# Two keys to a partition: regrouped V gathers, V table and weight transfers in a block-sparse attention and MoE kernel, with a new transfer model in its planner

## The chip, the cores and the metric

The kernel runs on one core of a Trainium2 chip. A core has the engines TensorE (PE in the profile, its weight loads PEld), VectorE (DVE), ScalarE (ACT), GpSimd (POOL) and SyncE (SP), each with its own queue of instructions that it works off in order, and 16 DMA engines that all queues of transfers share. The metric is the device time of one execution in microseconds, the lower the better; a kernel's time is the median of its runs.

## The reference

Block-sparse attention (4 batches, 8 heads, 768 positions of 64 values, blocks of 32 keys) is followed by a two-layer network on the joined heads:

```python
scores = (q @ k.T) / sqrt(64)            # per batch and head
mask   = |blk_i - blk_j| <= 1, or blk_i or blk_j is the first or the last block,
         or blk_j is one of the 3 sampled blocks of blk_i
attn   = softmax(where(mask, scores, -1e9));  a = attn @ v
x = a.transpose(0, 2, 1, 3).reshape(3072, 512)
h = x @ w_in                              # 512 x 2048
out = (h * sigmoid(beta * h)) @ w_out     # 2048 x 512, float32
```

All inputs are float32 in DRAM, the block numbers integers. Which keys a block of queries attends to is known only at run time, through the sampled blocks.

## The kernel before

**Attention.** Of 24 query blocks per batch the first and the last attend to all keys ("global"). The other 22 are worked in 11 pairs per batch, numbered 0 to 43. Each query block of a pair attends to 8 key blocks (first, last, three sampled, three neighbours), 256 keys. For a pair n the steps are, by their names in the code:

- kg (L521, POOL): copies the sampled K blocks from the transposed table KT into KG; kn (L525 on, POOL or DVE): copies first, last and neighbour blocks. 3 KG buffers.
- vv (L550, SP) reads the sampled block numbers into registers; vg (L582, SP) gathers V from a table VT in DRAM into VG, with 7 transfers to a pair (9 where a batch begins or ends). 4 VG buffers, so vg of pair n waits for av of pair n-4.
- vres (L589 on, POOL or DVE): in pairs 1 to 3 of a batch, copies the first and last block's V from pair 0's buffer.
- sc (L600, L610, PE): mask and scores, into two PSUM banks; mx (L621, DVE): row maxima; ex (L629, ACT): exponentials; rc (L635, DVE); nrm (L641, POOL or DVE): normalisation; tp (L653, PE): eight 128x128 transposes; ptv (L657, DVE): out of PSUM; av (L668, PE): times V; xv (L257, L259): out of PSUM into xT.

The global blocks have the same steps under gs, gm, ge, gr, gn, gt, gptv, gav and gx (L690 to L780).

**Tables.** For each batch K, Q and V are loaded (batch 0 by SP, L388, ahead of all; later batches by POOL, L443, into two staging buffers RAW), rearranged to fp16 by DVE (cast, vperm, perm), K and Q transposed by PE (trK, trQ, L463) and copied out of PSUM (evK, evQ). V goes back to DRAM as the table VT by SP: batch 0 in two halves of 512 B rows (vtab0.0, vtab0.1; L490), later batches at once in rows of 6 KB (vtab1 to 3; L494). Later batches are loaded in the order V, K, Q.

**MoE.** The 24 x 128 tokens are worked in 8 groups G of 256 or 512 tokens. Per group: h (L817, PE), 16 chunks of 128 hidden units by 4 matmuls; tanh (L823, ACT); stt (L828, DVE); y (L845, PE), 4 parts of 4 matmuls for each 128 tokens; oe (L263, ACT); od (output transfer, ACT). Weights are loaded by POOL, float32 to fp16 on the way, in 16 transfers: win (L417), 8 of 64 rows by 8 KB; wout (L423), 8 of 64 rows by 8 KB, four rows of w_out to a partition. All h wait for all eight win. The hidden units are therefore read at a stride of four: `w_in_v = w_in_sb[:, :, :].rearrange("x c (q p i) -> x c q i p", p=P, i=4)`.

**Order.** The kernel is written as tasks with an engine (or a choice of engines), a duration, dependencies and a priority. `Plan.run` plays them through in its own model when the kernel is built: whenever an engine is free it takes the ready task of the least priority number. The result is one order, and every engine's queue is that order cut down to the engine. In the model a transfer goes through one ring that serves one transfer after another (`ring_at = max(ring_at, end + 0.6) + t.dma`), transfers of SP and ACT also through 8 lanes in turn; a POOL load with `bulk` is held back while the ring is booked more than 3.2 us ahead. PSUM has 8 banks; `Plan(8, 4)` lets MoE tasks hold four of them while attention lasts. On the chip the order is fixed and every instruction waits for what it needs.

Of the kernel before, what the change touches and what calls it, by code (L numbers as in the profile page):

```python
# [22 lines left out]
class Task:  # L23
    def __init__(self, name, eng, dur, emit, deps=(), prio=0.0, lat=0.0,
                 opens=(), closes=(), moe=False, dma=0.0, slack=0.0, hw=0, bulk=None):
# [5 lines left out]
        self.slack, self.hw, self.bulk = slack, hw, bulk  # L31
        self.kind = name.rstrip("0123456789.")
        self.end = None


class Plan:
# [14 lines left out]
    def run(self):  # L51
# [16 lines left out]
        ring_at = 1.0  # L68
        lanes = [0.0] * 8
# [18 lines left out]
        while done < len(tasks):  # L88
            progress = False
            for e in engines:  # L90
# [3 lines left out]
                for t in waiting[e]:  # L94
# [7 lines left out]
                    if t.bulk is not None and ring_at > now + t.bulk + 1e-9:  # L102
                        continue
# [26 lines left out]
                if t.hw:  # L130
                    at = now
                    for _ in range(t.hw):
                        at = max(at, lanes[issued % 8]) + t.dur / t.hw
                        ring_at = max(ring_at, at + 0.4) + t.dma / t.hw
                        end = lanes[issued % 8] = ring_at + 0.9
                        issued += 1
                    free[e] = at
                elif t.dma:
                    ring_at = max(ring_at, end + 0.6) + t.dma
                    end = ring_at + 1.1  # L140
                t.start, t.end = now, end
                order.append(t)
                heapq.heappush(events, (end, seq, t))
                seq += 1
# [8 lines left out]
            for e in engines:  # L153
                nxt += [ready_at[t] for t in waiting[e] if ready_at[t] > now + 1e-9]
                nxt += [ring_at - t.bulk for t in waiting[e]
                        if t.bulk is not None and ring_at - t.bulk > now + 1e-9]
            nxt += [f for f, _ in bank_free if f > now + 1e-9]
            if not nxt:
                raise RuntimeError("plan is stuck: " + ", ".join(
                    t.name for e in engines for t in waiting[e]))  # L160
            now = max(now, min(nxt))
            while events and events[0][0] <= now + 1e-9:
# [3 lines left out]
                done += 1  # L166
                for s in succ.get(t, ()):
# [15 lines left out]
def kernel(  # L183
# [52 lines left out]
    VG = [sb(f"VG{i}", [P, 2, 2, D_MODEL]) for i in range(NVG)]  # L236
# [13 lines left out]
    plan = Plan(8, 4)  # L250
# [39 lines left out]
    t_sbl = add("sbl", "ACT", 0.5, emit_sbl, prio=-200, dma=0.3, hw=1)  # L290
# [46 lines left out]
    for part, f in enumerate((emit_mask0, emit_mask1, emit_mask2)):  # L337
# [9 lines left out]
    beta_row = osb[0][0:4, :]  # L347
    ident32 = t_sb[1][0:4, 0:8].bitcast(FP32)
    FQ = N_FFC // 4
    t_beta0 = add("beta", "ACT", 0.5, lambda: nc.scalar.dma_start(  # L350
        out=beta_row, in_=moe_beta.rearrange("(q x) -> q x", q=FQ)), prio=-140, dma=0.1, hw=1)
    t_id32 = add("id32", "DVE", 0.2, lambda: nc.vector.tensor_copy(
        out=ident32, in_=identity[0:4, 0:4]), deps=[t_ident], prio=-64)

    def emit_betaT():
        for i in range(4):
            nc.tensor.transpose(out=bank("beta")[:, i * FQ:(i + 1) * FQ],
                                in_=beta_row.rearrange("q (p i) -> q i p", i=4)[:, i, :], identity=ident32)
# [3 lines left out]
        out=beta_sb[:, :].rearrange("x (q i) -> x i q", i=4),  # L362
        in0=bank("beta")[:, 0:N_FFC].rearrange("x (i q) -> x i q", i=4),
# [22 lines left out]
    for i, (nm, t, dst) in enumerate((("K", k, K16), ("Q", q, Q16), ("V", v, None))):  # L386
        for f in range(2):
            tl = add(f"ld{nm}0.{f}", "SP", 0.47, lambda i=i, t=t, f=f: nc.sync.dma_start(  # L388
                out=stage_half(i, f) if i < 2 else v_stage[:, f * HH:(f + 1) * HH, :],
                in_=src6(t, 0, f * HH, HH)), prio=-80 + i * 2 + f, dma=2.0, hw=1)  # L390
# [17 lines left out]

    w_in_r = moe_w_in.rearrange("(c p) f -> c p f", p=P)
    w_out_r = moe_w_out.rearrange("(q p i) m -> q p (i m)", p=P, i=4)  # L410
    w_in_v = w_in_sb[:, :, :].rearrange("x c (q p i) -> x c q i p", p=P, i=4)
    t_win, t_wout = [], []
    THR = 3.2
    for c in range(4):
        for f in range(2):
            ps = slice(64 * f, 64 * f + 64)
            t_win.append(add(f"win{c}.{f}", "POOL", 0.85, lambda c=c, ps=ps: nc.gpsimd.dma_start(  # L417
                out=w_in_sb[ps, c, :], in_=w_in_r[c, ps, :]),
# [485 lines left out]
```

## Time and profile before

| | before |
|---|---|
| median of 3 runs | 324.45 us (322.56, 324.45, 332.4) |
| profiled execution | 323.59 us, of which the span 321.8 |
| mean granted TensorE clock | 0.929 |
| busy: PE, DVE, ACT, POOL | 280.7, 246.7, 216.8, 187.5 us |
| DMA | 42,211 packets, 43.97 MB |
| queue q1 (SP's transfers) | 27,760 packets, 25.71 MB, 27.1% of 16 engines |
| queue q0 (POOL's transfers) | 10,784 packets, 11.27 MB, 23.4% |
| V gathers, 32.0 KB each by the page's count | 268, median 2.6 us from issue to landing |

The page gives for each engine the busy tenths in 40 slices of the span; for each queue its packets, megabytes and the time that the packets took as a share of 16 engines' span; for each DMA issue the median time to landing. A timeline row reads: start, duration, engine, line, operation, out<-in, count, and in brackets the engine's idle time just before and what ended it. A row of the chain of work that ended last is start, duration, what. A group's row is busy time and the mean of one in ns, then idle time before it. TensorE's rows overlap, so its throughput is read from start to start. Every packet is also recorded in the trace with queue, size, start and duration; sizes are those stored for q0, whose loads turn float32 into fp16, and 16 packets of 4 bytes go with each transfer.

### The profile page before, as it was taken

How to read it: one execution, taken by the hardware profiler on the slowest of the kernel's cores; microseconds unless marked ns; L12 is line 12 of the kernel's file. 1: busy time of each engine (PE TensorE's matmuls, PEld its weight loads, DVE VectorE, ACT ScalarE, POOL GpSimd, SP SyncE). 2: the span in 40 equal slices, each digit the busy share in tenths (PEclk: the TensorE clock that was granted, in tenths of full speed). 3: DMA queues.
4: the chain of work that ended last, by engine and by line, in shares of the span. 5: the costliest groups of instructions: out<-in, count | busy, mean ns of one | idle time of the engine just before them, and what ended most of it. 6: DMA issues, size and time to landing. Idle time of an engine off the chain costs nothing.

```text
span 321.8 us, 10665 instructions
## 1 busy us (share of the span) xinstructions
PE 280.7 (87%) x3525; PEld 177.3 (55%) x3525; DVE 246.7 (77%) x572; ACT 216.8 (67%) x644; POOL 187.5 (58%) x528
## 2 busy tenths in 40 slices
PE   0845578989979699988979999999999999999994
PEld 0612366956755486556635656555665555554671
DVE  2996579878869989999987667999979975771060
ACT  1676435864968489789687669977679864772361
POOL 2479956848778456798966654756948453200000
PEclk9975557999979989999979999999999999999999
DMA  7889995998697586323777973335232333100201
GB/s 255 332 172 208 229 227 105 187 252 177 132 204 145 164 212 114 107 80 94 125 146 168 226 170 93 88 84 153 94 118 69 91 110 100 33 3 33 98 2 66
DMA packets 42211, 43.97 MB, mean 137 GB/s; under 512 B 6440, under 2 KB 37672, under 8 KB 42156
## 3 DMA queue, kind: packets, MB, share of 16 engines
q1 hardware_dynamic: 27760, 25.71, 27.1%
q0 software_dynamic: 10784, 11.27, 23.4%
q10 hardware_dynamic: 3612, 6.30, 5.4%
q8 instruction: 28, 0.46, 0.6%
q14 instruction: 27, 0.22, 0.2%
HBM read 45.10 MB, written 9.44 MB: 169 GB/s over the span
## 4 chain that ended last, share of the span: by engine, by line
PE 60%; DMA 14%; DVE 12%; ACT 6%; issue 3%; SPq 3%; POOL 1%; POOLq 0%; ACTq 0%; DVEq 0%
PE bank L845 22%; PE bank L817 21%; DMA VG<-VT 6%; PE bank L668 4%; PE bank L653 4%; DMA RAW<-in_k_dram 3%; DMA VT<-Vn 3%; SPq L582 3%; DVE ST L621 2%; ACT PP L629 2%; PE bank L463 2%; DVE g L828 2%; PE bank L610 2%; PE bank L600 2%; DMA sbl<-in_sampled_blocks_dram 1%
## 5 line engine op out<-in xcount | busy, mean ns | idle before, releaser
L641 POOL TENSOR_SCALAR PP<-PP,ST 128x256 f16<-128x256 f16 x168 | 81.3, 501 | 47.9 <-DVE ST L635 42.4
L629 ACT ACTIVATE PP<-bank,ST 128x256 f16<-128x256 f32 x176 | 81.6, 478 | 30.1 <-DVE ST L621 21.5
L817 PE MATMUL bank<-xT,w_in_sb 128*128 128x256 f16 (+1 forms) x512 | 97.1, 338 | 3.9 <-ACT PP L629 1.1
L845 PE MATMUL bank<-w_out_sb,g 128*128 128x512 f16 x384 | 90.9, 380 | 0.0
L828 DVE SCALAR_TENSOR_TENSOR g<-t,bank 128x512 f16<-128x512 f16 (+1 forms) x128 | 66.6, 546 | 22.1 <-ACT t L823 21.3
L823 ACT ACTIVATE t<-bank,beta_sb 128x512 f16<-128x512 f32 (+1 forms) x128 | 69.9, 589 | 14.3 <-PE bank L817 11.6
L817 PEld LDWEIGHTS <-w_in_sb 128*128 128x128 f16 x512 | 55.3, 116 | 30.1 <-issue 8.6
L521 POOL COPY KG<-KT 128x64 f32 x264 | 54.6, 256 | 24.6 <-PE bank L610 17.8
L621 DVE TENSOR_REDUCE ST<-bank 128x2 f32<-128x512 f32 x88 | 57.5, 678 | 7.5 <-PE bank L610 7.4
L845 PEld LDWEIGHTS <-g 128*128 128x128 f16 x384 | 34.7, 98 | 38.6 <-issue 4.1
L668 PE MATMUL bank<-PT,VG 128*128 128x64 f16 x704 | 31.8, 199 | 7.9 <-DMA VG<-VT 5.9
L668 PEld LDWEIGHTS <-VG 128*128 128x128 f16 x704 | 28.3, 102 | 16.5 <-issue 9.6
L629 ACT ACTIVATION_READ_ACCUMULATOR PP<-bank,ST 128x1 f32 x176 | 36.8, 209 | 0.0
L653 PE MATMUL bank<-identity,PP 128*128 128x128 f16 x352 | 30.9, 233 | 6.6 <-ACT xT L257 2.4
L653 PEld LDWEIGHTS <-PP 128*128 128x128 f16 x352 | 24.6, 104 | 15.9 <-issue 4.1
L657 DVE COPY PT<-bank 128x1024 f16<-128x1024 f16 x44 | 30.1, 684 | 4.1 <-PE bank L653 3.3
L259 DVE CAST xT<-bank 64x256 f16<-64x256 f32 (+1 forms) x52 | 20.6, 402 | 12.3 <-PE bank L668 7.5
L263 ACT ACTIVATE osb<-bank 128x512 f32<-128x512 f32 x24 | 14.4, 601 | 20.7 <-PE bank L845 20.7
L257 ACT CAST xT<-bank 64x256 f16<-64x256 f32 (+1 forms) x52 | 17.4, 346 | 15.4 <-DVE xT L259 6.3
L610 PE MATMUL bank<-KG,QT 64*32 64x256 f16 x704 | 20.9, 293 | 1.4 <-POOL KG L521 1.0
L726 ACT ACTIVATE PG<-bank,SG 128x384 f16<-128x384 f32 x32 | 18.4, 583 | 4.9 <-DVE SG L721 4.1
L600 PE MATMUL bank<-maskr,ones 64*32 64x192 f16 (+1 forms) x352 | 14.9, 272 | 5.7 <-ACT PP L629 5.5
(79 smaller groups left out, 256.6 us busy)
## 6 DMA issues: line engine op xcount, KB each, us to landing
VG<-VT SPq DMA_DIRECT2D x268, 32.0 KB, 2.6
VG<-VT SPq DMA_DIRECT2D x40, 192.0 KB, 2.9
out_dram<-osb ACTq DMA_DIRECT2D x20, 256.0 KB, 2.2
RAW<-in_v_dram POOLq DMA_DIRECT2D x6, 384.0 KB, 5.1
RAW<-in_k_dram POOLq DMA_DIRECT2D x6, 384.0 KB, 5.6
VT<-Vn SPq DMA_DIRECT2D x3, 768.0 KB, 6.1
RAW<-in_q_dram POOLq DMA_DIRECT2D x6, 384.0 KB, 6.5
w_in_sb<-in_moe_w_in_dram POOLq DMA_DIRECT2D x8, 256.0 KB, 5.9
```

Source lines behind the costliest of these rows:

```text
L521: nc.gpsimd.tensor_copy(out=kg32[:, g, :, (2 + r) * W:(3 + r) * W], in_=kt32[:, :, bass.ds(vals[3 * g + r], W)])
L610: nc.tensor.matmul(bk[u][hp * BLK:(hp + 1) * BLK, g * 256:(g + 1) * 256], lhsT=QT[b % 2][u * D:(u + 1) * D, hp, (i0 + g) * BLK:(i0 + g + 1 ...
L621: mx[n, u] = add(f"mx{n}.{u}", "DVE", 0.6, lambda n=n, u=u, sb_=sb_: nc.vector.tensor_reduce(out=sb_[:, 0, 2 * u:2 * u + 2], in_=bank(("S" ...
L629: nc.scalar.activation(out=pb[:, u, g, :], in_=bank(("S", n, u))[:, g * 256:(g + 1) * 256], func=AF.Exp, bias=sb_[:, 0, 2 * u + g:2 * u + ...
L641: (nc.vector if eng == "DVE" else nc.gpsimd).tensor_scalar(out=pb[:, u, g, :], in0=pb[:, u, g, :], scalar1=sb_[:, 2, 2 * u + g:2 * u + g + ...
L653: nc.tensor.transpose(out=o[:, s * P:(s + 1) * P], in_=pb[:, u, g, c * P:(c + 1) * P], identity=identity)
L657: ptv[n] = add(f"ptv{n}", "DVE", 0.61, lambda n=n: nc.vector.tensor_copy(out=PT[n % NPT], in_=bank16(("T", n))), deps=[tp[n]] + ([av[n - N ...
L668: nc.tensor.matmul(o[:, (g * NHP + hp) * 64:(g * NHP + hp + 1) * 64], lhsT=vgb[:, g, c, hp * P:(hp + 1) * P], rhs=pt[:, g, c, :, hp * BLK: ...
L817: nc.tensor.matmul(o[:, 0:TW], lhsT=w_in_v[:, c, f // 4, f % 4, :], rhs=xT[:, c, c0:c0 + TW], start=(c == 0), stop=(c == NHP - 1))
L823: lambda G=G, f=f, TW=TW, tt=tt: nc.scalar.activation(out=tt[:, 0:TW], in_=bank(("H", G, f))[:, 0:TW], func=AF.Tanh, bias=0.0, scale=beta_ ...
L828: lambda G=G, f=f, TW=TW, tt=tt, gg=gg: nc.vector.scalar_tensor_tensor(out=gg[:, f, 0:TW], in0=tt[:, 0:TW], scalar=1.0, in1=bank(("H", G, ...
L845: nc.tensor.matmul(o[:, :], lhsT=gg[:, f, s * P:(s + 1) * P], rhs=w_out_sb[:, f, :], start=(f == 0), stop=(f == N_FFC - 1))
```

## The change

- **V gathers.** A partition of VG now holds two neighbouring keys (2 KB in one row of the table) instead of one: a block of 32 keys takes 16 partitions, all 8 blocks of a query block stand in 128 partitions, and the second index of VG is the parity of the key instead of the lower or upper half. The same number of transfers per pair moves the same bytes. The transposes tp read the softmax at a stride of two, so that the keys' order fits. vres copies 32 partitions by 2,048 elements instead of 64 by 1,024.
- **V table.** Batch 0 is written by one transfer in rows of 6 KB, after both halves are cast.
- **Weights.** win: 8 transfers of 128 rows by 4 KB, the first half of the hidden units first; wout: 8 transfers of 128 rows by 4 KB, two rows of w_out to a partition. Chunks h.0 to h.7 wait for the first four win, h.8 to h.15 for the other four. Strides of four become two, also for beta.
- **Loads of later batches** come in the order K, Q, V; V uses K's staging buffer, after K is rearranged.
- **Planner.** Each queue of transfers (SP, ACT, POOL) has its own ring; the heads of the rings share the DMA engines packet by packet, in proportion to their packets' times. SP and ACT wait for a free lane of 8. POOL's `bulk` threshold is 2.2 us of its own ring's backlog. MoE tasks may hold five banks. With these the order of all engines changes. In the planned order vtab1 stands on SP ahead of the gathers of pairs 11 to 14, vtab2 ahead of those of pair 20, and permV1.1 on DVE ahead of stt1.6; all 12 vres go to DVE (before, 5 went to POOL).

```diff
-                 opens=(), closes=(), moe=False, dma=0.0, slack=0.0, hw=0, bulk=None):
+                 opens=(), closes=(), moe=False, dma=None, slack=0.0, bulk=None):
...
+class Rings:
+    START = {"SP": 0.4, "ACT": 0.4, "POOL": 1.0}
+    LAND = {"SP": 0.9, "ACT": 0.9, "POOL": 2.0}
...
+    def step(self):
+        live = [r for r in self.q if self.q[r] and self.q[r][0][0] <= self.at + 1e-9]
+        later = [self.q[r][0][0] for r in self.q if self.q[r] and r not in live]
+        total = sum(self.q[r][0][2] for r in live)
+        ends = [self.at + self.q[r][0][1] * total / self.q[r][0][2] for r in live]
+        return live, total, min(later + ends, default=None)
...
-                    if t.bulk is not None and ring_at > now + t.bulk + 1e-9:
+                    if t.bulk is not None and rings.backlog("POOL") > t.bulk:
+                        continue
+                    if t.dma and e != "POOL" and lanes[issued % 8] is not None:
                         continue
...
-    VG = [sb(f"VG{i}", [P, 2, 2, D_MODEL]) for i in range(NVG)]
+    VG = [sb(f"VG{i}", [P, 2, 2 * D_MODEL]) for i in range(NVG)]
...
-    plan = Plan(8, 4)
+    plan = Plan(8, 5)
...
-    w_out_r = moe_w_out.rearrange("(q p i) m -> q p (i m)", p=P, i=4)
-    w_in_v = w_in_sb[:, :, :].rearrange("x c (q p i) -> x c q i p", p=P, i=4)
+    w_out_r = moe_w_out.rearrange("(q p i) m -> p q (i m)", p=P, i=NI)
+    w_in_v = w_in_sb[:, :, :].rearrange("x c (q p i) -> x c q i p", p=P, i=NI)
     t_win, t_wout = [], []
-    THR = 3.2
...
-                out=w_in_sb[ps, c, :], in_=w_in_r[c, ps, :]),
-                deps=[tch], prio=-50 + 0.2 * c + 0.1 * f, dma=1.3, bulk=THR))
...
+    THR = 2.2
+    for f in range(2):
+        fs = slice(f * D_FF // 2, (f + 1) * D_FF // 2)
+        for c in range(NHP):
+            t_win.append(add(f"win{f}.{c}", "POOL", 0.6, lambda c=c, fs=fs: nc.gpsimd.dma_start(
+                out=w_in_sb[:, c, fs], in_=w_in_r[c, :, fs]),
+                deps=[tch], prio=-50 + 0.1 * len(t_win), dma=(8, 0.174), bulk=THR))
...
-            for nm, t, raw, dst in (("V", v, RAW[0], Vn[b % 2]), ("K", k, RAW[1], K16), ("Q", q, RAW[0], Q16)):
+            for nm, t, raw, dst in (("K", k, RAW[1], K16), ("Q", q, RAW[0], Q16), ("V", v, RAW[1], Vn[b % 2])):
...
-                vtab[0].append(add(f"vtab0.{f}", "SP", 0.45, lambda cs=cs, vt_rows=vt_rows: nc.sync.dma_start(
-                    out=vt_rows[:, :, cs], in_=Vn[0][:, :, cs]),
-                    deps=[vperm[0][f]], prio=-64, dma=1.3, hw=1))
+            vtab[0].append(add("vtab0", "SP", 0.45, lambda vt_rows=vt_rows: nc.sync.dma_start(
+                out=vt_rows, in_=Vn[0]), deps=vperm[0], prio=-64, dma=(8, 0.234)))
...
+        HB, W2 = BLK // 2, 2 * D_MODEL
+        def two(rows):
+            return rows.rearrange("(k t) m -> k (t m)", t=2)
...
             if i0 + 1 < NB - 2:
-                yield 0.6, lambda v: (
-                    vgb[BLK:P, :, 1, :],
+                yield 6, lambda v: (
+                    vgb[5 * HB:P, :, :],
                     bass.AP(tensor=vt.tensor, offset=vt.offset + (i0 - 1) * BLK * D_MODEL,
-                            ap=[[D_MODEL, 3 * BLK], [BLK * D_MODEL, 2], [1, D_MODEL]]))
+                            ap=[[W2, 3 * HB], [BLK * D_MODEL, 2], [1, W2]]))
...
-                for r, (c, s) in enumerate(((0, 2), (0, 3), (1, 0))):
-                    yield 0.1, lambda v, g=g, r=r, c=c, s=s: (
-                        vgb[s * BLK:(s + 1) * BLK, g, c, :], vt[bass.ds(v[3 * g + r], BLK), :])
+                for r in range(3):
+                    yield 1, lambda v, g=g, r=r: (
+                        vgb[(2 + r) * HB:(3 + r) * HB, g, :], two(vt[bass.ds(v[3 * g + r], BLK), :]))
...
-                h64 = src[0:2 * BLK, 0:1, 0, :]
-                copy_on(eng, vgb[0:2 * BLK, :, 0, :], h64.to_broadcast([2 * BLK, 2, D_MODEL]))
-            vres = add(f"vres{n}", {"POOL": 0.9, "DVE": 0.5}, None, emit_vres,
+                copy_on(eng, vgb[0:BLK, :, :], src[0:BLK, 0:1, :].to_broadcast([BLK, 2, 2 * D_MODEL]))
+            vres = add(f"vres{n}", {"POOL": 1.9, "DVE": 0.7}, None, emit_vres,
...
+            pk = pb[:, :, :, :].rearrange("x u g (k c) -> x u g c k", c=2)
...
-                                            in_=pb[:, u, g, c * P:(c + 1) * P], identity=identity)
+                                            in_=pk[:, u, g, c, :], identity=identity)
...
-                            lhsT=vgb[:, g, c, hp * P:(hp + 1) * P],
+                            lhsT=vgb[:, g, c * D_MODEL + hp * P:c * D_MODEL + (hp + 1) * P],
...
-            th = add(f"h{G}.{f}", "PE", 4 * (TW / 2400.0 + 0.003), emit_h, deps=xdeps + t_win,
+            th = add(f"h{G}.{f}", "PE", 4 * (TW / 2400.0 + 0.003), emit_h, deps=xdeps + t_win[f // 8 * 4:f // 8 * 4 + 4],
```

## The prediction

> **What bounds the kernel now.** I read the page's slices first, then the DMA queues, the timeline of each engine over the first 60 us, and the table by stretches.
>
> ```profile
> PE   0845578989979699988979999999999999999994
> DVE  2996579878869989999987667999979975771060
> PEclk9975557999979989999979999999999999999999
> DMA  7889995998697586323777973335232333100201
> q1 hardware_dynamic: 27760, 25.71, 27.1%
> q0 software_dynamic: 10784, 11.27, 23.4%
> ```
>
> A slice is 8.0 us. Three stages show. Up to slice 6 (54 us) TensorE is busy 0 to 8 tenths, its clock is at half from 20 to 51 us, and the DMA engines are full. From 54 to about 176 us TensorE and VectorE are both near full. From 176 us to the end TensorE has no holes: nothing but less matmul work shortens that stage, but whatever comes earlier moves all of it. The change does not touch the matmul count, so it pays only in the first two stages.
>
> What ends the waits in the first stage, by the timelines of VectorE and TensorE, the chain, and the DMA view from 15 to 55 us:
>
> ```profile
> 38.14 0.42 DVE L259 CAST xT<-bank 64x256 f16<-64x256 f32 x1 [3.09 <-PE bank L668]
> 36.11 0.53 PE L668 MATMUL bank<-PT,VG 128*128 128x64 f16 x7 [1.36 <-DMA VG<-VT]
> 37.25 0.79 PE L668 MATMUL bank<-PT,VG 128*128 128x64 f16 x8 [0.61 <-DMA VG<-VT]
> 47.34 0.56 PE L668 MATMUL bank<-PT,VG 128*128 128x64 f16 x7 [0.79 <-DMA VG<-VT]
> ...
> 17.85 8.90 DMA VT<-Vn
> 30.33 6.78 DMA VG<-VT
> ...
> q0 software_dynamic: 1453, 4.33, 60.8%
> q1 hardware_dynamic: 4210, 2.89, 24.9%
> VG<-VT SPq DMA_DIRECT2D x33, 32.0 KB, 5.2
> ```
>
> VectorE stands 3.09 us at the first output copy because av0 has no V; V is late because the V table took 8.90 us to write and the gathers behind it 6.78 us to land, against 2.6 us for such a gather over the whole run. Weights (q0) hold 60.8% of the engines, gathers and table 24.9%.
>
> **The V table.** The trace's packet records give medians of 27 ns for 512 B, 46 for 1,024, 65 for 1,536, 84 for 2,048 (the output's) and 238 for 6,144 on the queues of SP and ACT: about 8 ns and 37.5 ns a KB. Batch 0's table goes from 1,536 packets of 27 ns (41.5 us of engine time) to 128 of 238 ns (30.5): 11/16 = 0.7 us. It also leaves in one piece, behind the second cast, which has one K copy group fewer ahead of it (kn2, half of a row of 1.24 us: 0.6). The later tables, written this way, took 6.1 us to landing (median). So 17.8 - 0.6 + 6.1 = 23.3 us instead of 26.75: 3.4 us earlier.
>
> **The gathers.** Per pair 24 packets of 46 ns on each engine become 12 of 84: 1.10 to 1.01 us, 0.1 us per pair, 4.2 us over 44 pairs. The gain under load is larger: between two gather packets an engine serves weight packets of 324 ns; these read 8 KB; one that reads 4 KB is bounded by half of that (162) and by twice the output's 2,048 B packet (168); I take 165. Between 30 and 45 us the records show gathers at 0.25 of the engines and weights at 0.79: 2.2 gather packets to one weight packet. The first pair has 32 packets per engine now, 16 after: at the same ratio 32 x 46 + 14.5 x 324 = 6.2 us (6.7 observed) becomes 16 x 84 + 7.3 x 165 = 2.6; one to one, 16 x 249 = 4.0. Issue of its nine transfers stays (3.5 us). So pair 0 has V at 23.3 + 3.5 + 2.6 to 4.0, and an estimated 1 us for the landing: 30.4 to 31.8, not 37.1. By then tp2 (32.9 now) is the last thing ahead of av0: V is no longer what it waits for.
>
> **Weights.** 1,024 packets of 324 ns become 2,048 of 165: 20.7 to 21.1 us of all engines, +0.4. POOL still issues 16; a POOL transfer took 536 to 608 ns with 64 rows and 780 with 512, so 128 rows add at most 0.1 us each. Covered: the last weight landed near 48 us, the first second-layer matmul is at 66.0. The first-layer chunks 0 to 7 now need four transfers, not eight; all eight had landed by 36, so this gains nothing itself.
>
> **The residue copy (vres).** It now writes 32 partitions by 2,048, not 64 by 1,024.
>
> ```profile
> L259 DVE COPY VG<-VG 64x1024 f16<-64x1024 f16 x7 | 3.1, 452 | 0.0
> L259 POOL COPY VG<-VG 64x1024 f16<-64x1024 f16 x5 | 5.4, 1073 | 2.4 <-PE bank L668 2.4
> ```
>
> The new order puts all 12 on VectorE. Bounds per copy: 0.45 us (partitions free) and 0.90 (twice the elements); a 128x1536 copy took 0.61 to 0.90, so 0.80. 12 x 0.80 - 3.1 = +6.5 us. Four neighbour copies (0.4) and one normalisation (1.2) leave VectorE, so its sum grows by about 4 us and POOL's falls by 1 to 2.
>
> **Transposes of the softmax (L653)** read their weights at a stride of 2. Start to start the strided L745 (stride 6) and the packed L653 both run at 56 ns at full clock; only the load's latency differs, 125 against 98 ns. Nothing to 0.03 us per pair; I take nothing.
>
> **The new order.** Instruction lists of both kernels, weighted with the durations above: ahead of the first-layer matmul h0.0 VectorE has 4 us less to do (kn2, kn3, nrm1, nrm5, mx7 go elsewhere or later), TensorE 1.4 us less (tp5, tp6, av4 come after), POOL the same. POOL bounds it: K gather 7 ends at 12.45 + 28 us of its own rows + 2 of waits = 43, then scores, av3 and the copy, 46 to 47 instead of 53.7. But by the last element-wise step of the third MoE group (126 us now) the lists are level again: VectorE -0.8 us, TensorE within 2.4, ACT 0. So what is gained is the idle time removed, not the head start:
>
> - VectorE's idle behind missing V: 3.09 + 0.40 + 0.63 = 4.1 us (timeline to 54 us; 8.3 idle in all).
> - Batch 1's K is loaded first, not third: its wait of 1.81 us (71.60) goes, counted at half, 0.9, since V then comes last.
> - Lists: 0.8.
> - Against: waits in the new places; nearest are the six of 0.4 to 0.6 us that VectorE has in that stage for other causes. I take three, 1.5; bounds 0 and 4.
>
> Sum -4.1 - 0.9 - 0.8 + 1.5 = -4.3 us. From 176 us on, nothing hides or returns it: VectorE is busy 13 to 19 of 20 us there and its extra 4 us lie beside TensorE.
>
> **Batch 1's V** is the wait that is added. Its second load stands on POOL behind the K gathers of pairs 11 and 12, which wait for K's transposes; its cast on VectorE stands ahead of stt1.6; its table on SP stands ahead of the 30 gathers of pairs 11 to 14, which av11 to av14 wait for. From K ready: 2.4 (two K gathers) + 0.8 + 5.1 (load) + 0.8 (cast) + 6.1 (table) + 3.8 (nine issues) + 2.6 to 4.7 = 21.6 to 23.7, plus 1.5 to bring K out of PSUM. TensorE has 21.2 us of work between the last K transpose and av11, and took 27.4 for the like stretch before (72.56 to 99.94). 27 is over 25, so no stall; at no stalls of its own it would wait 2 to 4 us.
>
> The profiled execution took 323.59 us (span 321.8), close to the median of 324.45. 323.6 - 4.3 = **319.3, said as 319**; own range 316 to 323 (new waits 0 to 4, the copies 0.45 to 0.90). Two per cent, 6.5 us, is about what a measurement tells from no change.
>
> **Rivals.** (a) *The head start carries.* If VectorE's idle of 8.3 us before the first MoE group shrinks as the lists allow and TensorE is the limit all along: 53.7 - 46.5 = 7.2, less 1.4 deferred; plus K's wait 1.8 and av10's wait for V of 1.48 at 91.66: 9.1, **314.5**. For it: TensorE is busy 17 to 19 of 20 us. Against: VectorE 18 to 19.4 of 20 from 100 to 160. 0.27.
>
> (b) *V late in batch 1.* Stall 2 to 4 us at av11 and at stt1.6, eating the gain: **322 to 324**. 0.18.
>
> (c) *Slower: narrow gathers.* The six 16-partition moves of a pair put one packet on each engine, all into 16 partitions. If these partitions take data slower than the engines send it, a packet holds its engine. Price from rows: in quiet bursts of 32-row gathers (201 to 206 us) the slowest packets took 230 to 310 ns; if all 2 KB packets took 0.3, a pair costs 12 x 0.3 = 3.6 us instead of 1.0. Some 13 pairs fall where the DMA engines are 0.85 to 1.0 booked (20 to 105 us): +34 us on a stretch with 13 free, so up to 20 late, half of it on the path: **330**, between 326 and 340. It decides from 0.19 us a packet (13 x 12 x 0.11 = 17: the 13 free plus the 4 gained). Against: 32-row gathers' packets, on half as many partitions as a full load's, lie on the same line (46) as the wide ones. 0.12. The Trainium skill, "SBUF — State Buffer", section "Door 1: The DMA port swizzle", says DMA bandwidth depends on how many of 16 ports the partitions reach: 32 partitions reach 8, 16 reach 4. By its 436 GB/s for all ports a 32 KB gather would need an estimated 0.30 us, not 0.15, which would be case (c). The median of 46 ns shows no such limit at 8 ports; no run yet shows 4.
>
> (d) *Rows not joined*, gathers still in 1 KB packets: V table and order alone, **322**. Against: source and target rows are both contiguous, and the output's 2,048 B rows are single packets. 0.03. The forecast has 0.40.
>
> Faster by over 2% (under 317.1): (a) and a quarter of the forecast, 0.27 + 0.10 = 0.37. Within 2%: the rest of the forecast, (b) and (d), 0.30 + 0.18 + 0.03, less 0.07 for an order that goes wrong at a place I have not seen: 0.44. Slower: (c) and those 0.07: 0.19. Range 310 to 330: it leaves out half of (c) and the ends of (a).
>
> **What would show it.** q1 with about 17,700 packets, q0 about 11,800; a 2 KB gather packet at 84 ns; VT landed by 24; no V wait at av0; h0.0 near 46 to 48 us; VectorE some 4 us busier; av11 without a wait on VG. Wrong if gather packets take over 150 ns, if VT takes as long as now, if POOL waits long for K in batch 1, or if TensorE's holes between 60 and 176 us (12 us) grow by more than 4.

## The result

| | before | after |
|---|---|---|
| median | 324.0 us (runs made beside after) | 339.8 us |
| profiled execution | 323.6 us (span 321.8) | 337.9 us (span 336.1) |
| ratio after/before | | 1.041 [1.029, 1.052] |

The changed kernel is slower by 4%, 20.8 us above the forecast and 9.8 above the top of the range. Ratios leave out disturbed runs, which the medians contain, so in what follows ratios and traces are compared, not medians.

The slices and queues of the page of after, which answer to those of before:

```profile
PE   1746859998695999976999979994999998999994
DVE  2977777879795998994999658975859983673070
PEclk9975556999998799997999989998999999999999
DMA  7879996997775685147687843413323313400101
q1 hardware_dynamic: 17632, 25.71, 25.8%
q0 software_dynamic: 11808, 11.27, 23.2%
```

A slice is now 8.4 us. The queues have the packets that were forecast. What is new stands where nothing was expected: TensorE's row, which in before was full from 169 us on, has a 4 in its 28th slice (227 to 235 us). As a mean the granted clock is the same, 0.923 against 0.929.

The starts of some matmul tasks, in us from the start of the span, tell where the time goes. h2.0 is the first first-layer chunk of MoE group 2, h2.15 its last, h4.0 and h5.0 start groups 4 and 5, y7.1.3 is the last task of TensorE:

| | h0.0 | h1.0 | h2.0 | h2.15 | h4.0 | h5.0 | y7.1.3 |
|---|---|---|---|---|---|---|---|
| before | 53.7 | 78.9 | 107.0 | 126.7 | 192.2 | 234.6 | 316.2 |
| after | 50.0 | 75.9 | 103.1 | 127.2 | 195.8 | 247.7 | 330.9 |

Up to 103 us the change leads by 3 to 4 us, near the 4.3 that the forecast has as its net gain. Then it loses 4.4 by 127 us, 3.1 more by 196, 9.5 more by 248 and 1.6 to the end.

The chain of waits of after, at the first and the last of these places (start, duration, what):

```profile
99.04 0.50 ACT osb L309
99.56 3.03 DMA out_dram<-osb
102.61 0.32 SPq L634
...
104.61 0.32 SPq L634
104.92 0.05 issue
104.97 0.04 SPq L634
105.10 3.20 DMA VG<-VT
108.31 0.14 issue
108.44 0.58 PE bank L720 x8
```

```profile
228.28 2.10 DMA VG<-VT
230.39 0.03 issue
230.41 0.02 DVEq L305
230.43 0.04 issue
230.48 1.28 DVE VG L305 x2
```

At 108.44 TensorE's av12 waits for gathered V. That gather was issued only at 105.10, since SP's queue stood: its first gather was released by the landing of an *output* transfer, at 102.59, which ScalarE had issued at 99.56 and which has no data in common with it. At 230.48 VectorE's vres waits for a gather issued at 228.28; ahead of it SP's queue had stood from 224.02 to 227.85, until the output had landed that ScalarE issued at 225.81. So what does SP's queue wait for? The waits of SP, summed by releaser (us in total, times, longest), of before and then of after, the rows that name outputs:

```profile
SPq L899 <- DMA out_dram<-osb: 51.9, 4, 34.5
SPq L582 <- DMA out_dram<-osb: 8.1, 4, 4.2
```

```profile
SPq L634 <- DMA out_dram<-osb: 48.4, 14, 9.7
SPq L951 <- DMA out_dram<-osb: 42.0, 3, 28.0
```

L899 and L951 are the kernels' ends, where SP waits for all outputs, and mean nothing. L582 and L634 are the gathers: in before they stood for outputs 4 times and 8.1 us, in after 14 times and 48.4.

**Why a gather waits for an output.** The compiled programs show it. Every transfer of SP and of ScalarE signals its landing on one of eight semaphores, and these are dealt out in turn: in the one list in which the program names the instructions of all engines, the n-th such transfer takes semaphore n modulo 8, in each of the kernels here without exception. It is not issued before the transfer eight places earlier has landed. If that one is an output, SP waits for ScalarE to get to it and then for its landing, and behind the waiting gather stand all others, for SP works in order. The places are fixed when the program is compiled, and the engines' own orders don't tell them: the first outputs stand at 76, 84, 116, 124, 156, 170, 171, 218 in before, and at 73, 80, 96, 108, 140, 151, 153, 203 in after. The earlier an output stands among the gathers, the more SP, which runs ahead of the other engines, has to wait for it. Why the list comes out otherwise for the changed transfers is not shown here.

### The profile page after: what moved, and what is told of

The parts are those of the page before. It is cut to its first block, busy times and chain, and to the rows that moved or that the text cites. A ratio compares the mean times of both kernels' runs of the same rounds, so it can differ in the third digit from the quotient of the medians.

```text
span 336.1 us, 10650 instructions
## 1 busy us (share of the span) xinstructions
PE 286.8 (85%) x3523; PEld 173.5 (52%) x3523; DVE 245.4 (73%) x567; ACT 216.5 (64%) x644; POOL 189.5 (56%) x533
## 4 chain that ended last, share of the span: by engine, by line
PE 45%; DMA 20%; DVE 15%; ACT 10%; issue 5%; SPq 4%; ACTq 0%; DVEq 0%
PE bank L869 19%; PE bank L897 14%; DMA VG<-VT 13%; ACT PP L680 5%; DMA out_dram<-osb 5%; SPq L634 4%; DVE ST L672 4%; PE bank L720 4%; PE bank L705 3%; DVE g L880 2%; ACT t L875 2%; DVE PT L709 1%; DMA g<-in_k_dram 1%; DMA VT<-Vn 1%; PE bank L661 1%
## 5 line engine op out<-in xcount | busy, mean ns | idle before, releaser
L692 POOL TENSOR_SCALAR PP<-PP,ST 128x256 f16<-128x256 f16 x172 | 83.6, 502 | 63.8 <-DVE ST L686 56.1
L869 PE MATMUL bank<-xT,w_in_sb 128*128 128x256 f16 (+1 forms) x512 | 99.4, 341 | 2.3 <-DVE xT L305 1.5
L897 PE MATMUL bank<-w_out_sb,g 128*128 128x512 f16 x384 | 92.6, 382 | 0.3 <-DVE g L880 0.3
L869 PEld LDWEIGHTS <-w_in_sb 128*128 128x128 f16 x512 | 49.3, 102 | 34.6 <-issue 7.7
L568 POOL COPY KG<-KT 128x64 f32 x264 | 55.4, 258 | 18.0 <-PE bank L661 11.5
L672 DVE TENSOR_REDUCE ST<-bank 128x2 f32<-128x512 f32 x88 | 57.2, 680 | 10.4 <-PE bank L661 10.2
L705 PE MATMUL bank<-identity,PP 128*128 128x128 f16 x352 | 31.6, 233 | 8.8 <-DVE PTG L799 4.8
L305 DVE CAST xT<-bank 64x256 f16<-64x256 f32 (+1 forms) x52 | 20.9, 406 | 23.6 <-ACT xT L303 12.1
L789 POOL TENSOR_SCALAR PG<-PG,SG 128x768 f16<-128x768 f16 x13 | 12.0, 925 | 12.2 <-DVE SG L786 10.2
```

Of the source, the lines that this page charges most:

```text
L568: nc.gpsimd.tensor_copy(out=kg32[:, g, :, (2 + r) * W:(3 + r) * W], in_=kt32[:, :, bass.ds(vals[3 * g + r], W)])
L672: mx[n, u] = add(f"mx{n}.{u}", "DVE", 0.6, lambda n=n, u=u, sb_=sb_: nc.vector.tensor_reduce(out=sb_[:, 0, 2 * u:2 * u + 2], in_=bank(("S" ...
L692: (nc.vector if eng == "DVE" else nc.gpsimd).tensor_scalar(out=pb[:, u, g, :], in0=pb[:, u, g, :], scalar1=sb_[:, 2, 2 * u + g:2 * u + g + ...
L705: nc.tensor.transpose(out=o[:, s * P:(s + 1) * P], in_=pk[:, u, g, c, :], identity=identity)
L869: nc.tensor.matmul(o[:, 0:TW], lhsT=w_in_v[:, c, f // NI, f % NI, :], rhs=xT[:, c, c0:c0 + TW], start=(c == 0), stop=(c == NHP - 1))
L897: nc.tensor.matmul(o[:, :], lhsT=gg[:, f, s * P:(s + 1) * P], rhs=w_out_sb[:, f, :], start=(f == 0), stop=(f == N_FFC - 1))
```

## The experiments

"Behind an output" below counts the gathers and tables that take a semaphore directly after an output (12 in before, 19 in after). The first four runs were made before the semaphores were seen. Theory O: the new order loads V last, and V comes late. Theory G: the new layout of the gathers is slower. Theory P: the planner's choices as a whole.

Each diff is against the kernel that its paragraph starts from, cut to its core; `[by_name[w] for w in ORDER]` is put in short.

**New transfers in the old order** (from after). The order, the engines, the PSUM banks and the sequence V, K, Q are those of before, written out.

```diff
-    order = plan.run()
+    order = [by_name[w] for w in ORDER]        # the order planned for before, less vtab0.0
...
-            for nm, t, raw, dst in (("K", k, RAW[1], K16), ("Q", q, RAW[0], Q16), ("V", v, RAW[1], Vn[b % 2])):
+            for nm, t, raw, dst in (("V", v, RAW[0], Vn[b % 2]), ("K", k, RAW[1], K16), ("Q", q, RAW[0], Q16)):
```

> All transfers of the changed kernel (two keys to a partition, V table at once, weights in rows of 4 KB, the wider vres), but every engine's order, the choice of engines and the PSUM banks are those of the kernel before, and so is the load order V, K, Q. Theory O (the new order loses the time, V comes too late at the start of batches 1 to 3): 319 to 327 us, near the kernel before. Theory G (the narrow gathers of 16 partitions are slower): 332 to 340. Theory P (the new order as a whole, V or not): as O.

Measured: 339.56 us, ratio 1.054 [1.043, 1.064]. The whole loss is there without the new order. Outputs stand at 63, 76, 105, 115, 145, 156, 158, 203, with 20 gathers behind them. Its chain shows where TensorE's hole of 9.32 us ahead of 234.49 comes from:

```profile
219.87 0.61 ACT osb L452
220.50 2.00 DMA out_dram<-osb
222.51 0.33 SPq L774
...
225.31 0.36 SPq L774
225.73 2.90 DMA VG<-VT
228.70 0.09 issue
228.79 0.81 POOL VG L448
```

An output lands, SP issues the gathers behind it, one of them lands, and only then POOL can make the copies vres that the next pairs need.

**Old transfers in the new order**, the reverse: before's transfers and layout with the order written out from after, later batches loaded in the sequence K, Q, V.

```diff
-    order = plan.run()
+    order = [by_name[w] for w in ORDER]        # the order planned for after, vtab0.0 and vtab0.1 for vtab0
```

> The reverse: every transfer as in the kernel before (one key to a partition, V table of batch 0 in two halves, weights in rows of 8 KB), but the order, engines, banks and the load order K, Q, V of the changed kernel. Theories O and P: 334 to 344 us, with TensorE waiting at the first pairs of batches 1 to 3. Theory G: 320 to 328.

Measured: 324.06 us, ratio 1.001 [0.995, 1.007]. The order by itself costs nothing and brings nothing. SP stood 2.7 us for outputs at gathers.

**V not waited for** (from after, its order written out). The tables of the later batches are written from w_out_sb, which is there early: the kernel leaves V out of them, with the same bytes and packets.

```diff
-                out=vt_rows, in_=Vn[b % 2]), deps=vperm[b], prio=pr + 5, dma=(8, 0.234), slack=1.0)]
+                out=vt_rows, in_=w_out_sb[:, 0:J, :]), deps=vperm[b], prio=pr + 5, dma=(8, 0.234), slack=1.0)]
```

> The changed kernel in its own order, fixed, but the V tables of batches 1 to 3 are written from the second layer's weights, which lie ready, in place of V: the same bytes and packets, no wait for V's load and rearrangement, so the attention of batches 1 to 3 is computed with wrong values. Theory O: the holes before av11 and av12 (2.5 and 2.8 us), av20 (3.1) and tp32 (4.9) go, 324 to 329 us. Theories G and P: 334 to 339, as the changed kernel.

Measured: 339.72 us, ratio 1.055 [1.047, 1.064]; SP's waits for outputs at gathers 47.7 us.

**V loaded first again** (from after), with the order planned anew.

```diff
-            for nm, t, raw, dst in (("K", k, RAW[1], K16), ("Q", q, RAW[0], Q16), ("V", v, RAW[1], Vn[b % 2])):
+            for nm, t, raw, dst in (("V", v, RAW[0], Vn[b % 2]), ("K", k, RAW[1], K16), ("Q", q, RAW[0], Q16)):
```

> The changed kernel with the loads of batches 1 to 3 in the order V, K, Q and the staging buffers as in the kernel before; the planner orders it anew. Theory O: 318 to 328 us. Theory P: 332 to 340, since the planner's new transfer model and its fifth MoE bank stay. Theory G: 332 to 340.

Measured: 342.92 us, ratio 1.060 [1.044, 1.075]; waits 51.3 us. Theories O and P had missed both kernels with exchanged orders, and O misses these two as well: V's place in the loads does not matter. G was left, and with it the theory formed now, L: the loss is SP's queue standing for outputs. To tell them apart, the next kernels keep every engine's instructions and their order and change only the places of the outputs in the list.

**The two-key gathers alone** (from before, in its order).

```diff
-                yield 0.6, lambda v: (
-                    vgb[BLK:P, :, 1, :],
+                yield 0.600, lambda v: (
+                    vgb[5 * HB:P, :, :],
...
-                copy_on(eng, vgb[0:2 * BLK, :, 0, :], h64.to_broadcast([2 * BLK, 2, D_MODEL]))
+                copy_on(eng, vgb[0:BLK, :, :], src[0:BLK, 0:1, :].to_broadcast([BLK, 2, 2 * D_MODEL]))
```

> The kernel before in its own fixed order, engines and banks, with the two-key gathers alone (VG, the restores L309-like as 32x2048, the strided transposes); V table in two halves and weights in 2 KB rows as before. Every transfer of SP and ScalarE takes one of eight completion semaphores in turn, in the order of the one list in which the compiled program names the instructions of all engines, and it can't be issued until the transfer eight places earlier has landed. In this list the two-key gathers move the outputs forward: the first output stands behind 61 transfers of SP instead of 74, the others 10 to 15 earlier too, and 20 gathers instead of 12 take a semaphore after an output. Theory L (the loss is SP's queue standing at a gather until an output has landed): 338 to 341, with SP's waits on outputs among the gathers near 47 us instead of 8. Theory G (two-key gathers are slower by themselves, or their copies): 338 to 341 too. Theory W (it was the weights or the V table): 324.

Measured: 344.86 us, ratio 1.061 [1.051, 1.071]; waits 44.9 us. This part of the change is enough for the loss.

**The new transfers in the old order, outputs later in the list.** Each output is bound, in the list only, to stand behind the last gather that the written order names ahead of it. No engine waits for anything by this.

```diff
+                    if is_dma and t.name.startswith("od"):
+                        tc.add_manual_dep(i, sp, dep, reason="list")     # sp: last gather; dep: NoSync, no wait
```

> layout_old_order (every transfer of the changed kernel in the fixed order of before, 339.6) with the same instructions in the same order on every engine, and one thing else: in the list each output stands behind the last gather that the written order issues ahead of it, so that the outputs stand 4 to 23 places later and 13 gathers instead of 20 take a semaphore after an output, most of them gathers that are issued long after. No wait is taken from an engine but that on the semaphores' turn. Theory L: 321 to 326, SP's waits on outputs among the gathers under 12 us. Theory G: 338 to 341, as before.

Measured: 321.38 us, ratio 0.987 [0.978, 0.996]. From a ratio of 1.054 to 0.987 with the same instructions in the same order on each engine. The only waits of SP for outputs that its trace has are those of the end (L1114), and ScalarE has one at an output for a gather:

```profile
SPq L1114 <- DMA out_dram<-osb: 51.5, 3, 37.5
ACT PG L918 <- DMA VG<-VT: 2.9, 1, 2.9
```

**Before, outputs earlier in the list.** The reverse: gathers are bound to stand behind outputs, at about the places that the two-key gathers give.

```diff
+                    if is_dma and od:
+                        tc.add_manual_dep(i, od, dep, reason="list")     # i: a gather; dep: NoSync
```

> The kernel before, its transfers and its layout untouched and the same instructions in the same order on every engine; only the place of the outputs in the list is moved forward to about where the two-key gathers put them (69, 77, 106, 118, 146, 157, 158, 204 and so on instead of 76, 84, 116, 124, 156, 170, 171, 218), so that 18 gathers instead of 12 take a semaphore after an output. Theory L: 332 to 341, with 25 us or more of SP's waits on outputs among the gathers. Theory G: 324.

Measured: 332.68 us, ratio 1.022 [1.011, 1.032]; waits 22.6 us. Slower with not one transfer changed; a third of two_key_alone's loss at half of its waits, with places less early than those of the two-key gathers (first output at 69, not 63). The size is uncertain: the ratio rests on two runs, 326.86 and 331.53 us, and the first, whose trace this is, had a granted clock of 1.0 throughout, where before had 0.72 in its first 54 us. G has no account of the loss.

**After, outputs later in the list**, by the same edit as above.

> The changed kernel, the same instructions in the same order on every engine; only in the list each output stands behind the last gather that the written order issues ahead of it (first output at place 78 instead of 73, then 88, 103, 114, 162, 172 instead of 80, 96, 108, 140, 151). Theory L: 318 to 326, SP's waits on outputs among the gathers under 12 us instead of 48; if the rest of the prediction holds, near 319. Theory G: 338 to 341.

Measured: 322.84 us, ratio 0.999 [0.994, 1.005], span 321.4 against 336.1. The loss of after is gone; 14.7 us of span went with SP's waits for outputs. Not all of that is idle time. Between h0.0, at 50.0 us in both, and h5.0 TensorE works off the same 2,352 matmuls; its holes are 7.6 us shorter in all, and its busy time is 171.3 us instead of 176.7. The second part goes with the granted clock. In this stretch after runs at half clock up to 55.8 us, for 6.8 us from 107.0 and for 3.4 us each from 154.8, 199.2 and 233.3; after_outs_placed does so up to 53.9 and for 6.8 us from 135.9. These are 12.1 us more at half clock, an estimated 6 us of work. Past 60 us each such piece lies beside a hole of TensorE (they end at 108.44, 154.78, 199.18 and 233.65 in after, at 136.47 in after_outs_placed), but not every hole has one (86.78 in after). So a wait at SP can cost more than the hole that it makes; that the hole brings the half clock is read from this and not tested by a run.

**The control: before, outputs placed in the same way.**

> The kernel before, the same instructions in the same order on every engine; only in the list each output stands behind the last gather that the written order issues ahead of it (76, 84, 116, 124, 163, 179, 180 and so on instead of 76, 84, 116, 124, 156, 170, 171). The control for the two kernels with placed outputs. Of before's 8.1 us of SP's waits on outputs among the gathers little stays. If the gathers in before have slack where they wait, 323 to 326 and the 321.4 of layout_old_order_outs_placed is the worth of the new transfers (about -1%); if the placing is worth it by itself, 319 to 322 and the new transfers are worth nothing.

Measured: 327.15 us, ratio 1.015 [1.002, 1.028], profiled 323.82 against 323.59. Placing is no gain by itself; by ratio it is a small loss. The two profiled times are alike though one has 8.1 us of waits and the other none, so before's waits lay in slack.

**Weights and V table alone**, in before's order, gathers with one key to a partition.

```diff
-    w_out_r = moe_w_out.rearrange("(q p i) m -> q p (i m)", p=P, i=4)
+    w_out_r = moe_w_out.rearrange("(q p i) m -> p q (i m)", p=P, i=NI)
...
-                    out=vt_rows[:, :, cs], in_=Vn[0][:, :, cs]),
+                out=vt_rows, in_=Vn[0]), deps=vperm[0], prio=-64, dma=1.9, hw=1))
```

> The kernel before in its fixed order with weights in 4 KB rows (each half of the first layer waited for by itself) and batch 0's V table written at once, gathers and restores as before (one key to a partition). The list of the program moves the outputs forward by 1 to 6 places only (70, 81, 110, 118, 154, 167, 169, 212). Theory L: 322 to 327, with at most 15 us of SP's waits on outputs among the gathers. The prediction's step for the V table (3.4 us earlier) and the weights (+0.4, hidden): 321 to 324. If half of the loss came from weights or table after all: 330 or more.

Measured: 322.6 us, ratio 0.999 [0.994, 1.005]. Waits of 16.2 us for outputs, twice before's, cost nothing here. A likely reason is that the four buffers of V let SP issue gathers well ahead of their use; it is not shown.

**Outputs later still.** Ahead of each output stand all gathers whose buffer is free by the written order. In the old order with the new transfers:

> layout_old_order_outs_placed with the outputs later still in the list: ahead of each output stand all gathers whose buffer is free by the written order (first outputs at place 100, 101, 130, 146 instead of 73, 81, 113, 121), the order of each engine unchanged. An output now takes a semaphore after gathers that may be issued late. If what is left of the waits on outputs still costs, 317 to 320; if nothing is left of that kind, as placed, 320 to 323; if ScalarE now stands at outputs until gathers have landed, 324 to 330.

Measured: 340.78 us, ratio 1.063 [1.051, 1.074]. And the changed kernel:

> after_outs_placed with the outputs later still in the list, in the same way (first outputs at place 90, 91, 123, 131 instead of 78, 88, 103, 114). As for the old order: 317 to 320 if waits on outputs still cost there, 320 to 324 if none is left, 324 to 330 if ScalarE stands at outputs behind gathers. With after_outs_placed it also tells the new order from the old one: the prediction's gain by the order would put this 3 to 5 us under layout_old_order_outs_pulled.

Measured: 342.89 us, ratio 1.068 [1.060, 1.077]. The worst of the three cases that were written down, and far worse than written. SP no longer waits for any output at its gathers; ScalarE now stands at outputs for gathers. The waits of ScalarE for gathers in the first of the two, and a piece of its chain:

```profile
ACT xT L446 <- DMA VG<-VT: 22.9, 3, 17.0
ACT PP L820 <- DMA VG<-VT: 6.2, 1, 6.2
ACT PG L918 <- DMA VG<-VT: 0.7, 1, 0.7
```

```profile
86.23 2.14 DMA VG<-VT
88.45 0.38 ACTq L1055
88.93 0.10 ACT xT L446
```

L1055 is the issue of an output: it waits until the gather eight places earlier has landed, and the copy xT behind it on ScalarE waits too. In the profile this reads as a copy waiting for V, which it never touches. So the turn of the semaphores ties both queues to each other, and each output has a window of places: too early and SP stands, too late and ScalarE does.

**Outputs placed by measured times.** Still open was where the forecast gain of 4.3 us had gone, since after_outs_placed only equals before. In it ScalarE stood 3.9 us at one output (131 us), and TensorE 2.5 us behind it. Each output was put midway between the two ends of its window, from the issue times in the traces of the placed kernels.

```diff
+    PLACE = [78, 85, 96, 108, 148, 161, 163, 211, 218, ...]      # SP transfers ahead of each output
```

> The changed kernel, the same instructions in the same order on every engine; each output's place in the list is taken from the issue times in after_outs_placed: midway between the earliest place at which the gather eight places later still finds the output landed and the latest at which the output finds the gather eight places earlier landed (80, 88, 100, 113, 154, 168, 171, 220 and so on; the output at 162, for which ScalarE stood 3.9 us, goes to 154). If that stall is what ate the gain: 318 to 321, TensorE's hole of 2.5 us near 136 us gone and the second-layer end of batch 1's stage (h4.0) near 188.5 instead of 190.9. If the new order has nothing to give: 321.5 to 325.

Measured: 323.99 us, ratio 1.001 [0.995, 1.008]. The stall at 131 us went, and the next output took its place. Its chain and, from TensorE's timeline, what followed:

```profile
136.67 4.84 DMA VG<-VT
141.51 0.02 issue
141.53 0.33 ACTq L1062
```

```profile
143.04 0.84 PE L901 MATMUL bank<-KT,QT 64*32 64x384 f16 x15 [4.50 <-ACT PP L824]
```

The same for the old order with the new transfers:

> The new transfers in the fixed order of before, outputs placed in the same way from the issue times in layout_old_order_outs_placed (73, 82, 112, 121, 155, 171, 175, 223 and so on); ScalarE stood 2.9 us at an output in that one, with no hole of TensorE behind it. Expected 319.5 to 322. If the new order is worth its predicted 4.3 us, after_outs_timed is 2 to 4 us under this one; if it is worth nothing, within 1.5 us.

Measured: 324.51 us, ratio 1.002 [0.997, 1.008]; ScalarE stood 8.0 us at two outputs. That is above what was written down, and midway places did no better than the first ones here. Nor is the new order ahead of the old one by 2 to 4 us, as it would be if it were worth its 4.3: the ratios are 1.001 and 1.002.

Then the one stall of after_outs_timed was taken out, by two places:

```diff
-    PLACE = [78, 85, 96, 108, 148, 161, 163, 211, 218, ...]
+    PLACE = [78, 85, 96, 108, 148, 157, 157, 211, 218, ...]
```

> after_outs_timed with two places in the list changed: the two halves of the output of ScalarE at 137 us stand at 164 and 166 instead of 168 and 171, behind gathers issued 2 to 4 us earlier. If the stall of 3.9 us there ate the gain: TensorE's hole of 4.50 us near 143 us shrinks to under 1.5, h4.0 starts near 188 instead of 191.1, and the profiled span is 317 to 319 instead of 320.5, the median 2 to 3 us under that of after_outs_timed on a like chip; ratio to before 0.985 to 0.995. If another wait takes its place, nothing changes: ratio 0.995 to 1.008, and the order has nothing to give.

Measured: 322.58 us, ratio 0.991 [0.985, 0.997], within the better of the two cases; but not by the way written down. The hole at 143 us shrank from 4.50 to 1.11, and h3.0 came 2.9 us earlier (140.9). Then ScalarE stood 2.9 us at another output, TensorE 2.31 at 176.83, and h4.0 was at 191.7, no earlier than in after_outs_timed (191.1). The two profiled spans, 321.1 and 320.5, don't show a gain either. So the gain by ratio is small, and I don't claim its cause.

All runs beside each other. "SP" is SP's wait for outputs at its gathers, "ScalarE" the wait of ScalarE for gathers, in us; for after_outs_timed the trace names POOL for ScalarE's 4.37 us, which the chain above gives to the gather:

| kernel | behind an output | SP | ScalarE | ratio |
|---|---|---|---|---|
| before | 12 | 8.1 | 0 | 1 |
| order_old_layout | 13 | 2.7 | 2.6 | 1.001 |
| weights_and_table_alone | 15 | 16.2 | 0 | 0.999 |
| before_outs_placed | 12 | 0 | 0 | 1.015 |
| before_outs_early | 18 | 22.6 | 0 | 1.022 |
| after | 19 | 48.4 | 0 | 1.041 |
| layout_old_order | 20 | 46.9 | 0 | 1.054 |
| v_not_awaited | 19 | 47.7 | 0 | 1.055 |
| v_first | 17 | 51.3 | 0 | 1.060 |
| two_key_alone | 20 | 44.9 | 0 | 1.061 |
| layout_old_order_outs_placed | 13 | 0 | 2.9 | 0.987 |
| after_outs_placed | 12 | 0 | 3.9 | 0.999 |
| after_outs_timed | 15 | 1.9 | 4.4 | 1.001 |
| layout_old_order_outs_timed | 16 | 3.0 | 8.0 | 1.002 |
| after_outs_timed_twice | 15 | 0 | 2.9 | 0.991 |
| layout_old_order_outs_pulled | 14 | 0 | 29.8 | 1.063 |
| after_outs_pulled | 15 | 0 | 20.5 | 1.068 |

Every kernel with over 40 us of SP's waits, or 20 or more of ScalarE's, is 4 to 7% slower; every one with at most 17 and 8 lies between 0.987 and 1.015. The count of gathers behind an output alone does not sort them (17 in v_first, 18 in before_outs_early): when they are due decides.

## Why the prediction was wrong, step by step

**The step that failed is "Against: waits in the new places ... I take three, 1.5; bounds 0 and 4."** It looked for new waits on VectorE, priced by VectorE's own small ones. The new waits are on SP's queue, 14 instead of 4 and 40.3 us more, and they cost 14.7 us of span (336.1 less 321.4 with the outputs placed), holes and half clock together. SP's in-order queue had been counted where a step was moved past it, for batch 1's table; that the other queue's outputs stand in its turn of semaphores was not. No rival had it either. The range's upper half held a slower case, (c), with a fitting size (330, up to 340) and another mechanism, which did not happen (below).

**The gain of 4.3 us did not reach the end.** This is the second error: with SP's waits gone the profiled execution is 323.1 us, not 319.3. The early lead is there: with the outputs placed, h0.0 is 3.7 us earlier than before, h2.0 4.0 and h2.15 3.9. At h4.0 1.3 are left, at the end 0.1. With the outputs placed, the step "from 176 us on, nothing hides or returns it" was nearly right: 1.2 us go between 192 and 240 us, where TensorE is busy for 46.7 of 48 us against 48.0 in before. The rest, 2.6 us, was lost ahead of that, between 123 and 191 us, and 2.5 us of it is TensorE's hole behind ScalarE's stall at an output; when the stalls were moved, others came. Whether the new order would keep its lead with no such stall is open: no run of it was without one. Four pairs of kernels with the new transfers differ by the order, with the loads' sequence that belongs to it, and by their outputs' places; their ratios, new and old, are 1.041 and 1.054, 0.999 and 0.987, 1.001 and 1.002, 1.068 and 1.063. Their difference changes its sign, so no gain by the order is shown. What the new transfers are worth is open too: in the old order they gave 0.987, about the size of the whole forecast, with one set of places and 1.002 with another.

**The V table**: forecast landed at 23.3, measured 22.1 (its second cast ended at 17.46, 4.63 us before). Right, and 1.2 us better.

**The gathers**: forecast for pair 0's V 30.4 to 31.8. The last of its gathers landed at 32.44, 0.6 us past that, against 37.1 to 37.4 in before, and av0 at 33.84 has no wait for V, as forecast. But the way there was wrong. The engine time of all gathers was to fall by 4.2 us; it went from 61.3 to 61.6. The medians are 46 and 84 ns as in the forecast; the means are 56.4 and 113.2. From the table's landing to that of pair 0's V it took 10.3 us (from 22.1), in before 10.4 to 10.7 (from 26.75), where the forecast's terms make 7.1 to 8.5: almost nothing of the gathers' saving came, and the table's lead did it.

**Weights**: forecast 165 ns a packet and +0.4 us; measured 173 as median, 197.8 as mean, 25.3 us against 22.7. The last weight packet is at 54.2 instead of 47.2 us. The cover held: the first second-layer matmul stands at 64.7 (66.0 in before).

**vres**: forecast 0.80 us on VectorE, measured 0.68; all 12 are there:

```profile
L305 DVE COPY VG<-VG x12: 651/682/879, 32.5 to 238.6; 32x2048 f16<-32x2048 f16 x12
```

(ns: least, median, most.) VectorE's sum was to grow by 4 us; it is 245.4 instead of 246.7. POOL's is 189.5 instead of 187.5, where 1 to 2 less were forecast. No effect of either sum is seen. Where the copies stand matters more: VectorE stood 5.8 us for a gather ahead of those at 230.48.

**The strided transposes**: mean 233 ns in both kernels, as forecast: nothing.

**The order**: h0.0 forecast at 46 to 47, measured at 50.0 (53.7 before), so half of the head start.

**Batch 1's V**: no wait at av11, as forecast. The waits for V in after at av10 (86.78, 1.50 us), av12 (108.44, 2.49) and av20 (154.78, 2.98) are of gathers; the middle one is the chain shown above.

**Rivals.** (a) did not happen: not even the lead at h0.0 was carried on. (d) did not: the packet counts show the rows joined. (b) did not: av11 has no wait, and v_not_awaited is as slow as after. (c) was right in sign, near in size and wrong in cause: the loss vanishes with the narrow gathers in place (layout_old_order_outs_placed). Of the gathers of 32 KB that stand alone in the record of packets, 64 into 16 partitions took 0.37 us as median from first to last packet (0.28 to 0.48 for the middle four fifths), and 48 into 32 partitions in before 0.39 (0.32 to 0.45). The Trainium skill, "SBUF — State Buffer", section "Door 1: The DMA port swizzle", ties bandwidth to the ports that the partitions reach; for transfers as small as these the traces show no difference between the 16 partitions of after and the 32 of before.

**"What would show it"** had growing holes of TensorE between 60 and 176 us as the sign of an error. By that measure it did not come: TensorE's idle time in this window went from 11.6 to 14.2 us, less than the 4 more that were named, though from h0.0 to h4.0 after takes 145.8 us and before 138.5. The largest hole came later, 4.76 us ahead of 233.65, where the prediction had none.

## What to carry to other kernels

Before a change of transfers is priced, in programs like these look at the compiled list: which transfer stands eight places ahead of each gather and each output, and which of the two engines is earlier at that point. A change that regroups transfers can move these places though every engine's own order stays, and the queue that then stands can be one whose order the diff does not touch. In a profile, read SP's and ScalarE's waits by releaser, and when an instruction waits for a transfer whose data it never reads, suspect the semaphore; the cure is the place of the transfer in the list, with a window that has two ends.

## What the runs showed of the hardware beyond that

- Packets of twice the size did not save engine time under load: 17,408 packets of 1 KB took 61.3 us of 16 engines in before, 8,704 of 2 KB 61.6 in after (58.8 to 61.3 and 57.9 to 63.1 over all traces here). By the medians they would have saved (twice 46 against 84 ns); the difference is in the slow tenth (60 and 182 ns at the 90th percentile).
- Weight packets that read 4 KB took 173 ns as median, more than half of the 324 ns of those that read 8 KB, and 25.3 us in all instead of 22.7.
- The last stage is rigid: from h5.0 to y7.1.3 the 17 traces here take 81.4 to 83.3 us, so all but about 2 us of the differences in span are made before h5.0.
